# Pack products by four blocks, the last routing behind group 0, and the expert groups on two shared PSUM banks

## The chip, the cores and the metric

The kernel runs on one core of one Trainium2 chip. The metric is the device time of one execution in microseconds (us), as the median of several runs. Engines are named as in the profile: PE is TensorE's matmul stream and PEld its weight loads, DVE is VectorE, ACT is ScalarE, POOL is GpSimd, SP is SyncE, whose queue issues most DMAs. PSUM has eight banks of 128 x 512 fp32.

## What is computed

Three layers in a chain, the first from q, k, v and 32 packed queries p (8 batches, 8 heads, 576 positions, width 64):

```
p_packed = softmax(p k^T / 8) v;  x = softmax(q p_packed^T / 8) p_packed    # 4608 tokens x 512
h = relu(x @ w_in);  x = (h * h) @ w_out               # 512 -> 2048 -> 512, weights are float64
logits = x @ w_gate + modality_bias[modality_id]
e = argmax(logits);  gate = softmax(logits)[e]
out[token] = gate * (relu(x[token] @ w1[e]) @ w2[e])   # 8 experts, 512 -> 1024 -> 512
```

All of it is held to fp32 accuracy: most operands are split in two parts, hi and lo, and each product is made as hi*hi + hi*lo + lo*hi, three matmuls.

## The kernel before, in words

**Front.** The packed attention `att1` (L288 and after) runs over 16 pairs (batch, half of the heads). A front loop near the end of the file advances up to four of them by a step each tick, and every other tick pulls `conversions()`, which loads a 1 MB piece of the float64 weights, turns it into fp32 with one ACT and four DVE operations, and, for `w_out`, splits it by ACT and POOL. Pieces not converted in the front are converted in the main loop's unit 0, one per tick.

**Main loop.** Twelve units `u` of 384 tokens, in each 16 ticks `f` (128 hidden columns of 2048). A tick is `layer1` (matmuls at L455 on attention weights `a2T` and a block of the packed product), the activations (L464 to L468), and `layer2` of the tick before (L475, nine or so matmuls into three `acc` banks). The packed product is `pw(b, q)` (L359): for batch `b` and columns 256q to 256q+255 of `w_in`, eight fp32 matmuls of 64 rows, 32 columns and 256 moving columns (L365) into a pair of PSUM banks named `two`, then one ACT copy (L376) and one DVE subtraction (L377) that leave two blocks in `ring`, a ring of 20 blocks, 18 of them in one tile and two in `rtail`. `ahead()` says after which tick which `pw` is written. While the units run, `tail(u)` (L490 to L513) forms the gate logits of a unit, 24 DVE operations at L496, and `route()` (L522 to L647) puts its tokens on expert lists: its last step makes `om` and `od` on DVE and, from them, `pl` on PE (L640), one matmul per tile of 128 tokens. `tables()` (from L653) turns lists into the row indices of the gathers and scatters.

**Groups.** Nine groups of 512 tokens, each of one expert. `gathered(g)` fetches the rows by four indirect DMAs on POOL's queue (`xg`, L731) and turns them by 16 PE transposes (`tr`, L745) in PSUM banks "t"; ACT (L748) and DVE (L749) split them into `xt`. `group(g)` makes eight blocks `h` (L765, 12 matmuls of 128x512 each), evacuated by ACT (L775) and DVE (L776) into `ht`; then four output tiles `o` (L787, 24 matmuls each) into "acc" banks, scaled on DVE (L796) and scattered from POOL's queue (L798). Meanwhile SP loads the next expert's weights into two `raw` buffers (L708, L716) and ACT and DVE split them (L701, L702): four pieces of 1024 columns for w1 (`wb`) and eight of 512 for w2 (`ring`). Every third `h` block sits in the bank "h" of one pool, the others in the two banks of pool `h3`; three accumulators, two "t" banks, these three: all eight are used.

**Order.** The code is written with generators, but the Tile framework's scheduler sets the final order of each engine by its own simulated timeline and the priorities in the code; each engine then works strictly in that order.

Of the kernel before, what the change touches and what calls it, by code (L numbers as in the profile page):

```python
# [20 lines left out]
P = 128  # L21
# [5 lines left out]
def tile_pack_attention_moe_moe2(  # L27
# [191 lines left out]
    def conversions():  # L219
# [12 lines left out]
        for n in range(2):  # L232
            load(n)
        for n, (kind, u) in enumerate(CV):
            raw = raw_of(n).rearrange("p (f t) -> p f t", t=2)
# [23 lines left out]
    def bank(tag, name):  # L259
        if tag == "acc":  # L260
            return held["acc_p"].tile([P, 512], F32, tag="acc", name=name)
        return held["ps"].tile([P, 512], F32, tag=tag, name=name, bufs=held["bufs"][tag])

# [94 lines left out]

    def pw(b, q):  # L359
        ph = banks("pw")  # L360
        for g, j in ((0, 0), (2, 1), (2, 0), (0, 1), (1, 0), (3, 1), (3, 0), (1, 1)):
            c = g // 2
            o = (j + c) % 2 * NPK
            r = (2 * (g % 2)) * NPK + o
            nc.tensor.matmul(  # L365
                ph[r : r + NPK, c, : 2 * P],
                pp32[j * D : (j + 1) * D, b, g, o : o + NPK],
                w_in[q // 4 * HP + g][j * D : (j + 1) * D, q % 4 * 2 * P : (q % 4 + 1) * 2 * P],
                start=True,
                stop=True,  # L370
                tile_position=(j * D, r),
            )
        t = blocks(block(b, 2 * q), 2)
        src = ph[:, :, : 2 * P].rearrange("p c (k f) -> p k c f", k=2)
        hi = t[:, :, 0]
        nc.scalar.activation(out=hi, in_=src, func=AF.Copy)  # L376
        nc.vector.tensor_tensor(out=t[:, :, 1], in0=src, in1=hi.bitcast(F32), op=ALU.subtract)  # L377

# [344 lines left out]
    def gathered(g):  # L723
# [18 lines left out]
        for c in range(NDC):  # L742
            tp = bank("t", "tr")
            for t in range(NTT):
# [8 lines left out]
    def group(g, more):  # L753
# [4 lines left out]
        for f in range(NFE):  # L758
            if f % 2 == 0:
                pull(w2s)  # L760
            ph = bank("h", "h3") if f % 3 == 2 else held["h3"].tile([P, 512], F32, tag="h3", name="h3")
            i = 0
# [80 lines left out]
    def ahead(pair, k, f):  # L843
        late = {2 * m + 1: m + 2 for m in range(6)}
        if k == 0:
            b, q = (0, late.get(f)) if pair == 0 else (0, None)
            if q is not None:
                pw(b, q)
            b, q = 2 * pair + 1, {12: 0, 14: 1}.get(f)
        elif k == 1:  # L850
            b, q = 2 * pair + 1, late.get(f)
        else:
            b, q = 2 * pair + 2, (late | {0: 0, 2: 1}).get(f)
        if q is not None and b < B:
            pw(b, q)

# [85 lines left out]
    for i in range(len(quads) + 4):  # L942
        if i < len(quads):
            runs.append(att1(i))
        for r in (runs if i < 4 else runs[:1] + runs[:0:-1]):
            next(r)
        if i >= 4:
            runs.pop(0)
        if i % 2 and i < len(quads):
            pull(cv)  # L950
        if i == 6:
            bg = [att2(0)]
        pull(bg)
        if i >= len(quads):
            pw(0, i - len(quads)) if i < len(quads) + 2 else None
    pull(bg, 100)
# [10 lines left out]
    second_layer()  # L967
    other = [tail(NUN - 1), route(NTL - UT, NTL)]
    pull(other, 100)
    st3.close()  # L970
    held["h"] = ctx.enter_context(tc.tile_pool(name="h", bufs=NFE, side="left"))
    tables(G_A, G_MAX)

    for g in range(G_ALL):
        with tc.high_priority(offset=200 if g == 0 else 0):
            group(g, g + 1 < G_ALL)
    total = nc.values_load(ge_i[0:1, G_MAX : G_MAX + 1], min_val=0, max_val=G_MAX)

# [62 lines left out]
```

## Time and profile before

| | us |
|---|---|
| median of 3 runs (lowest, highest) | 1341.38 (1341.34, 1341.47) |
| the profiled execution: its own time | 1340.63 |
| its span, first to last instruction | 1338.8 |
| PE busy in it | 1252.5 (94%) |
| DVE, ACT, POOL busy | 773.2, 559.3, 175.5 |

The trace divides the span into the front (0 to 107 us), the main loop (to 870 us, when the last `acc` matmul ends) and the groups (870 to 1339 us, the first of them already mixed with the last ticks of the main loop). Read it from PE: a stretch in which PE is busy throughout gets shorter only by less PE work, a stretch with PE idle gets shorter by removing the wait. The lines called waits say how long an engine stood idle and which instruction released it.

### The profile page before, as it was taken

What the parts mean: (1) busy time and instruction counts of PE and PEld (TensorE: products, weight loads), DVE (VectorE), ACT (ScalarE), POOL (GpSimd) and SP (SyncE); (2) the same over time, 40 slices, a digit from 0 to 9 for tenths busy, and PEclk for the clock granted to TensorE, in tenths of its full rate; (3) what the DMA queues carried; (4) which work ended last, traced back from release to release, by engine and by line L of the source; (5) the groups of instructions that cost most, each with busy time, mean ns of one, the idle gap of its engine ahead of it and who ended that gap; (6) DMA issues with size and microseconds to landing.
All of it is one profiled execution on the core that took longest, in us unless ns stands there. A gap on an engine that the chain in (4) does not pass through costs nothing.

```text
span 1338.8 us, 19978 instructions
## 1 busy us (share of the span) xinstructions
PE 1252.5 (94%) x7572; PEld 985.0 (74%) x7572; DVE 773.2 (58%) x2008; ACT 559.3 (42%) x1061; POOL 175.5 (13%) x225
## 2 busy tenths in 40 slices
PE   5768999999999999999999999995999999999995
PEld 3546677778877878887778778874778778778774
DVE  5786654577375737764774778687243443443431
ACT  3445644554444555444444546523132332332320
POOL 4214610001000000000000010100122122122101
PEclk8787999999999999999999999997989999999997
DMA  9973300001000000010001021515142442443310
GB/s 356 369 251 127 118 17 33 9 25 33 33 33 17 24 25 33 16 49 9 26 25 41 1 88 39 157 56 177 41 144 79 149 154 77 149 159 107 122 56 34
DMA packets 56634, 115.79 MB, mean 86 GB/s; under 512 B 4432, under 2 KB 24016, under 8 KB 55376
## 3 DMA queue, kind: packets, MB, share of 16 engines
q1 hardware_dynamic: 50768, 95.25, 21.1%
q0 software_dynamic: 5760, 19.17, 4.3%
q8 instruction: 61, 1.00, 0.3%
q14 instruction: 45, 0.37, 0.1%
HBM read 95.24 MB, written 19.17 MB: 85 GB/s over the span
## 4 chain that ended last, share of the span: by engine, by line
PE 84%; DVE 6%; DMA 5%; ACT 2%; issue 2%; POOL 1%; POOLq 0%; SPq 0%; ACTq 0%; DVEq 0%
PE acc L475 29%; PE ph L455 16%; PE h L765 14%; PE o L787 13%; PE pw L365 4%; DMA xg<-x_d,idx_g 3%; PE s L410 2%; DMA wraw<-in_moe_w 1%; PE tr L745 1%; PE s L302 1%; PE pv L334 1%; PE ta L324 1%; DVE wi L244 1%; DVE ring L702 1%; PE ta L437 1%
## 5 line engine op out<-in xcount | busy, mean ns | idle before, releaser
L475 PE MATMUL acc<-wb,ghl 128*128 128x512 f32 x1728 | 447.7, 401 | 0.2 <-ACT ghl L466 0.2
L475 PEld LDWEIGHTS acc<-wb,ghl 128*128 128x128 f32 x1728 | 314.7, 189 | 80.8 <-issue 9.9
L455 PE MATMUL ph<-a2T,ring 128*128 128x384 f32 (+1 forms) x1392 | 237.3, 312 | 1.3 <-DVE pp L352 0.7
L455 PEld LDWEIGHTS ph<-a2T,ring 128*128 128x128 f32 x1392 | 208.2, 191 | 25.5 <-issue 12.8
L787 PE MATMUL o<-ring,ht 128*128 128x512 f32 x864 | 219.8, 400 | 3.5 <-ACT ht L775 3.2
L765 PE MATMUL h<-xt,wb 128*128 128x512 f32 x864 | 219.0, 402 | 0.5 <-ACT xt L748 0.5
L496 DVE SCALAR_TENSOR_TENSOR rows<-rows,wgb 128x512 f32<-128x512 f32 x288 | 199.4, 692 | 4.7
L765 PEld LDWEIGHTS h<-xt,wb 128*128 128x128 f32 x864 | 164.9, 192 | 40.8 <-ACT xt L748 1.1
L787 PEld LDWEIGHTS o<-ring,ht 128*128 128x128 f32 x864 | 161.5, 189 | 41.9 <-ACT ht L775 4.1
L464 ACT ACTIVATE r<-ph 128x384 f32<-128x384 f32 x192 | 94.2, 491 | 213.5 <-PE ph L455 198.1
L468 DVE TENSOR_TENSOR ghl<-r,ghl 128x384 fp32r<-128x384 f32 x176 | 98.6, 560 | 116.9 <-ACT ghl L466 113.2
L430 POOL TENSOR_TENSOR e<-e,sm 128x256 f32<-128x256 f32 x36 | 28.2, 782 | 597.6 <-ACT ghl L466 233.2
L466 ACT ACTIVATE ghl<-r 128x384 fp32r<-128x384 f32 x192 | 100.7, 524 | 5.7
L465 ACT ACTIVATE r<-r 128x384 f32<-128x384 f32 x192 | 100.9, 525 | 5.1
L796 DVE TENSOR_SCALAR wgb<-o,gt 128x512 f32<-128x512 f32 x36 | 27.0, 750 | 122.9 <-PE o L787 110.4
L776 DVE SCALAR_TENSOR_TENSOR ht<-h,ht 128x512 fp32r<-128x512 f32 x72 | 48.4, 687 | 56.3 <-ACT ht L775 56.3
L748 ACT ACTIVATE xt<-tr 128x512 fp32r<-128x512 f32 x36 | 21.4, 597 | 141.2 <-PE tr L745 136.5
L798 POOL DMA_INDIRECT out<-wgb,idx_s x36 | 38.8, 1078 | 297.5 <-DVE wgb L796 249.6
L775 ACT ACTIVATE ht<-h 128x512 fp32r<-128x512 f32 x72 | 40.9, 594 | 77.7 <-PE h L765 73.7
L365 PE MATMUL pw<-wi,pp 64*32 64x256 f32 x1024 | 70.3, 392 | 3.2 <-ACT eb L315 2.4
L376 ACT ACTIVATE ring<-pw 128x512 fp32r<-128x512 f32 x58 | 34.5, 596 | 86.8 <-PE ph L455 82.6
L702 DVE TENSOR_TENSOR wb<-wraw,wb 128x1024 fp32r<-128x1024 f32 x36 | 44.1, 1224 | 35.9 <-ACT wb L701 34.5
(186 smaller groups left out, 1092.2 us busy)
## 6 DMA issues: line engine op xcount, KB each, us to landing
wraw<-in_moe_w SPq DMA_DIRECT2D x72, 512.0 KB, 3.6
x_d<-rows SPq DMA_DIRECT2D x12, 792.0 KB, 3.5
qT<-in_q SPq DMA_DIRECT2D x36, 256.0 KB, 2.8
eb<-in_v SPq DMA_DIRECT2D x16, 512.0 KB, 8.0
eb<-in_k SPq DMA_DIRECT2D x11, 576.0 KB, 8.1
wgb<-in_moe_w_out SPq DMA_DIRECT2D x6, 1024.0 KB, 4.9
wgb<-in_moe_w_in SPq DMA_DIRECT2D x5, 1024.0 KB, 9.0
ec<-in_moe_w_in SPq DMA_DIRECT2D x3, 1024.0 KB, 8.3
```

Source lines behind the costliest of these rows:

```text
L365: nc.tensor.matmul(ph[r : r + NPK, c, : 2 * P], pp32[j * D : (j + 1) * D, b, g, o : o + NPK], w_in[q // 4 * HP + g][j * D : (j + 1) * D, q ...
L455: nc.tensor.matmul(ph[:, off : off + n], t[:, x, c, :], a[:, y, c, off : off + n], start=(i == 0), stop=(i == 3 * NPC - 1),)
L464: nc.scalar.activation(out=r, in_=ph, func=AF.Relu)
L465: nc.scalar.activation(out=r, in_=r, func=AF.Square)
L466: nc.scalar.activation(out=hl[:, 0], in_=r, func=AF.Copy)
L468: eng.tensor_tensor(out=hl[:, 1], in0=r, in1=hl[:, 0].bitcast(F32), op=ALU.subtract)
L475: nc.tensor.matmul(acc[t], hl[:, x, t * P : (t + 1) * P], w_out(f)[:, y, :], start=(f == 0 and x == 0 and y == 0), stop=(f == NF - 1 and x ...
L496: nc.vector.scalar_tensor_tensor(out=junk, in0=row[:, t, :DM], scalar=1.0, in1=wgb[:, e], op0=ALU.mult, op1=ALU.mult, accum_out=one)
L702: nc.vector.tensor_tensor(out=t[:, 1, :], in0=raw, in1=t[:, 0, :].bitcast(F32), op=ALU.subtract)
L765: nc.tensor.matmul(ph, half1(g % 2, c)[:, x, f * P : (f + 1) * P], xs[c][:, y, :], start=(i == 0), stop=(i == 3 * NDC - 1),)
L776: nc.vector.scalar_tensor_tensor(out=h[:, 1, :], in0=ph, scalar=0.0, in1=h[:, 0, :].bitcast(F32), op0=ALU.max, op1=ALU.subtract)
L787: nc.tensor.matmul(po, hs[f][:, x, t * P : (t + 1) * P], second(f)[:, y, :], start=(i == 0), stop=(i == 3 * NFE - 1),)
```

## The change

1. `conversions()` stops once (`yield`) behind its first two loads, and the front loop pulls it at tick 1 and at the odd ticks from 3 to 18, instead of every odd tick to 15.
2. `pw(b, f, n)` takes `n` blocks of 128 columns. `ahead()` asks for four at a time for the even batches and for the first four blocks of odd ones, for two elsewhere. A call whose blocks cross from the ring's main tile into `rtail` evacuates in two parts. The calls go from 64 to 44 (20 of four blocks, 24 of two).
3. `route()` of the last tokens and the `tables()` of the later groups are written behind group 0 instead of ahead of it. `tail()` of the last unit stays ahead.
4. Every `h` block takes one of the two banks of `h3`; the transposes `tr` of groups 1 to 8 take a bank of `h3` as well instead of a "t" bank.

```diff
@@ conversions
         for n in range(2):
             load(n)
+        yield
@@ bank
+        if tag == "h3":
+            return held["h3"].tile([P, 512], F32, tag="h3", name=name)
@@ pw
-    def pw(b, q):
+    def pw(b, f, n):
...
-                ph[r : r + NPK, c, : 2 * P],
+                ph[r : r + NPK, c, : n * P],
...
-                w_in[q // 4 * HP + g][j * D : (j + 1) * D, q % 4 * 2 * P : (q % 4 + 1) * 2 * P],
+                w_in[f // 8 * HP + g][j * D : (j + 1) * D, f % 8 * P : (f % 8 + n) * P],
...
-        t = blocks(block(b, 2 * q), 2)
-        src = ph[:, :, : 2 * P].rearrange("p c (k f) -> p k c f", k=2)
-        hi = t[:, :, 0]
-        nc.scalar.activation(out=hi, in_=src, func=AF.Copy)
-        nc.vector.tensor_tensor(out=t[:, :, 1], in0=src, in1=hi.bitcast(F32), op=ALU.subtract)
+        i = block(b, f)
+        for k0, k1 in ((0, n),) if i + n <= MOST or i >= MOST else ((0, MOST - i), (MOST - i, n)):
+            t = blocks(i + k0, k1 - k0)
+            src = ph[:, :, k0 * P : k1 * P].rearrange("p c (k f) -> p k c f", f=P)
+            hi = t[:, :, 0]
+            nc.scalar.activation(out=hi, in_=src, func=AF.Copy)
+            nc.vector.tensor_tensor(out=t[:, :, 1], in0=src, in1=hi.bitcast(F32), op=ALU.subtract)
@@ gathered
-            tp = bank("t", "tr")
+            tp = bank("h3" if g else "t", "tr")
@@ group
-            ph = bank("h", "h3") if f % 3 == 2 else held["h3"].tile([P, 512], F32, tag="h3", name="h3")
+            ph = bank("h3", "h3")
@@ ahead
-        late = {2 * m + 1: m + 2 for m in range(6)}
+        two = {2 * m + 1: (2 * m + 4, 2) for m in range(6)}
+        four = {4 * m + 3: (4 * m + 4, 4) for m in range(3)}
         if k == 0:
-            b, q = (0, late.get(f)) if pair == 0 else (0, None)
-            if q is not None:
-                pw(b, q)
-            b, q = 2 * pair + 1, {12: 0, 14: 1}.get(f)
+            b, q = 2 * pair + 1, {12: (0, 4)}.get(f)
+            if pair == 0 and f in (1, 5, 9):
+                b, q = 0, (f + 3, 4)
         elif k == 1:
-            b, q = 2 * pair + 1, late.get(f)
+            b, q = 2 * pair + 1, two.get(f)
         else:
-            b, q = 2 * pair + 2, (late | {0: 0, 2: 1}).get(f)
+            b, q = 2 * pair + 2, (four | {0: (0, 4)}).get(f)
@@ the front loop
-        if i % 2 and i < len(quads):
+        if i % 2 and 3 <= i < len(quads) + 3:
+            pull(cv)
+        if i == 1:
             pull(cv)
...
-        if i >= len(quads):
-            pw(0, i - len(quads)) if i < len(quads) + 2 else None
+        if i == len(quads):
+            pw(0, 0, 4)
@@ behind the main loop
-    other = [tail(NUN - 1), route(NTL - UT, NTL)]
-    pull(other, 100)
+    pull([tail(NUN - 1)], 100)
...
-    tables(G_A, G_MAX)
...
             group(g, g + 1 < G_ALL)
+        if g == 0:
+            pull([route(NTL - UT, NTL)], 100)
+            tables(G_A, G_MAX)
```

The lines shift by up to eight in the new file: `tr` L745 is L750, `h` L765 is L770, `ht` L776 is L781, `o` L787 is L792, the scaling L796 is L801, `pl` L640 is L645, the weight split L702 is L707, `xt` L749 is L754.

What that makes of the order shows first on PE, at the last routing's matmuls `pl` (of `om` and `od`). Before, they stand between group 0's last `o` and group 1's first `h`, with `tr` of group 1 behind the first of them (the numbers in names are buffers):

```order
L787 MATMUL o_9027<-ring,ht 128x512 x17
L640 LDWEIGHTS om
L640 MATMUL pl<-od,om 128x184
L745 MATMUL tr<-ident,xg 128x128 x4
L640 LDWEIGHTS om
L640 MATMUL pl<-od,om 128x184
L640 LDWEIGHTS om
L640 MATMUL pl<-od,om 128x184
L765 MATMUL h_9071<-xt,wb_1114 128x512
```

And after, on PE, where all of group 1's transposes and its first `h` blocks have gone by, between its third and fourth `h` block:

```order
L770 MATMUL h_8913<-xt,wb_1103 128x512 x12
L792 MATMUL o_9034<-ring,ht 128x512
L792 MATMUL o_9075<-ring,ht 128x512
L792 MATMUL o_9124<-ring,ht 128x512
L792 MATMUL o_9034<-ring,ht 128x512 x2
L792 MATMUL o_9075<-ring,ht 128x512 x2
L792 MATMUL o_9124<-ring,ht 128x512 x2
L645 LDWEIGHTS om
L645 MATMUL pl<-od,om 128x184
L645 LDWEIGHTS om
L645 MATMUL pl<-od,om 128x184
L770 MATMUL h_8935<-xt,wb_1103 128x512 x12
```

The routing's matmuls, which stood ahead of every `h` of group 1, have moved behind three of its `h` blocks and nine `o` products.

The second place is PE at the passage from a group to the next. Before, the last group's output `o_9377` and the next group's three first blocks `h_9421`, `h_9437`, `h_9459` are mixed, and the transposes of the group after that stand among them:

```order
L787 MATMUL o_9377<-ring,ht 128x512 x22
L765 MATMUL h_9421<-xt,wb_1113 128x512
L765 MATMUL h_9437<-xt,wb_1113 128x512
L765 MATMUL h_9459<-xt,wb_1113 128x512
L787 MATMUL o_9377<-ring,ht 128x512
L765 MATMUL h_9421<-xt,wb_1113 128x512 x2
L765 MATMUL h_9437<-xt,wb_1113 128x512 x2
L765 MATMUL h_9459<-xt,wb_1113 128x512 x2
L745 MATMUL tr<-ident,xg 128x128 x4
L787 MATMUL o_9377<-ring,ht 128x512
L745 MATMUL tr<-ident,xg 128x128 x4
L787 MATMUL o_9596<-ring,ht 128x512 x2
```

And after, at the same passage on PE, the last output tile `o_9515` runs through in one piece, the last four transposes follow, then the next group's `h` blocks one by one:

```order
L792 MATMUL o_9384<-ring,ht 128x512
L792 MATMUL o_9425<-ring,ht 128x512
L750 MATMUL tr<-ident,xg 128x128 x4
L792 MATMUL o_9474<-ring,ht 128x512
L750 MATMUL tr<-ident,xg 128x128 x4
L792 MATMUL o_9515<-ring,ht 128x512 x24
L750 MATMUL tr<-ident,xg 128x128 x4
L770 MATMUL h_9559<-xt,wb_1103 128x512 x12
L770 MATMUL h_9575<-xt,wb_1103 128x512 x12
L792 MATMUL o_9734<-ring,ht 128x512 x2
L792 MATMUL o_9775<-ring,ht 128x512 x2
```

The transposes of one gather no longer stand ahead of work that needs nothing from it.

The third place is DVE at that passage, which frees the `h` banks. Before:

```order
L702 TENSOR_TENSOR ring<-wraw,ring 128x512 x6
L776 SCALAR_TENSOR_TENSOR ht<-h_9421,ht 128x512
L796 TENSOR_SCALAR wgb<-o_9377,gt 128x512
L776 SCALAR_TENSOR_TENSOR ht<-h_9437,ht 128x512
L776 SCALAR_TENSOR_TENSOR ht<-h_9459,ht 128x512
L702 TENSOR_TENSOR ring<-wraw,ring 128x512 x2
L702 TENSOR_TENSOR wb_1114<-wraw,wb_1114 128x1024
L776 SCALAR_TENSOR_TENSOR ht<-h_9475,ht 128x512
```

After, on DVE, at the passage from group 0 to group 1:

```order
L754 TENSOR_TENSOR xt<-tr,xt 128x512 x2
L707 TENSOR_TENSOR ring<-wraw,ring 128x512 x4
L801 TENSOR_SCALAR wgb<-o_9165,gt 128x512
L754 TENSOR_TENSOR xt<-tr,xt 128x512
L707 TENSOR_TENSOR ring<-wraw,ring 128x512 x4
L781 SCALAR_TENSOR_TENSOR ht<-h_9209,ht 128x512
L781 SCALAR_TENSOR_TENSOR ht<-h_9225,ht 128x512
L707 TENSOR_TENSOR wb_1103<-wraw,wb_1103 128x1024 x2
L781 SCALAR_TENSOR_TENSOR ht<-h_9247,ht 128x512
```

The first `ht` of a group, which frees its `h` bank, now stands behind the scaling of the last output tile and four splits of the next weights, where before it stood ahead of that scaling.

## Rows read from the trace of the kernel before

**Rows 1.** The page: span, and the chain that ended last, by engine.

```profile
span 1338.8 us, 19978 instructions
...
PE 84%; DVE 6%; DMA 5%; ACT 2%; issue 2%; POOL 1%; POOLq 0%; SPq 0%; ACTq 0%; DVEq 0%
```

**Rows 2.** Table by stretch: window, length, busy PE PEld DVE ACT POOL, PEclk, DMA share, GB/s.

```profile
120.00:150.00 30.00, 29.36 (x188) 22.12 (x187) 21.61 (x28) 20.53 (x40) 21.28 (x16) 1.00 0.26 88
...
200.00:400.00 200.00, 200.00 (x1274) 157.93 (x1273) 124.86 (x375) 96.98 (x199) 7.52 (x9) 1.00 0.08 25
```

**Rows 3.** The same table by groups: the last routing, then two of seven periods.

```profile
915.00:930.00 15.00, 2.25 (x9) 1.46 (x9) 13.64 (x32) 5.86 (x7) 0.17 (x1) 0.53 0.54 167
...
947.03:1001.32 54.29, 51.03 (x217) 40.82 (x216) 18.86 (x27) 14.30 (x24) 8.93 (x12) 0.94 0.27 88
...
1241.50:1293.25 51.75, 51.23 (x225) 40.98 (x224) 22.15 (x30) 16.21 (x25) 5.26 (x5) 1.00 0.32 105
```

**Rows 4.** PE's waits, 870 to 1293 us: instruction, releaser, total us, times, longest.

```profile
PE pl L640 <- DVE od L632: 15.0, 2, 14.0
PE tr L745 <- DMA xg<-x_d,idx_g: 14.0, 9, 2.0
```

**Rows 5.** Timeline of PE from the last layer-2 matmuls into group 1: start, us, instruction.

```profile
868.32 2.27 PE L475 MATMUL acc<-wb,ghl 128*128 128x512 f32 x9
873.31 1.20 PE L787 MATMUL o<-ring,ht 128*128 128x512 f32 x4 [2.72 <-ACT ht L775]
...
947.03 1.33 PE L765 MATMUL h<-xt,wb 128*128 128x512 f32 x5
```

**Rows 6.** Timeline of PE at a boundary between groups.

```profile
979.88 0.60 PE L745 MATMUL tr<-ident,xg 128*128 128x128 f32 x4
980.23 5.37 PE L787 MATMUL o<-ring,ht 128*128 128x512 f32 x22
...
990.57 0.44 PE L745 MATMUL tr<-ident,xg 128*128 128x128 f32 x2 [1.98 <-DMA xg<-x_d,idx_g]
992.29 0.69 PE L745 MATMUL tr<-ident,xg 128*128 128x128 f32 x2 [1.28 <-DMA xg<-x_d,idx_g]
...
994.49 4.44 PE L765 MATMUL h<-xt,wb 128*128 128x512 f32 x12
```

**Rows 7.** A piece of the critical chain: start us, us, what.

```profile
894.06 14.00 PE o L787 x60
```

**Rows 8.** Timeline of PE: fp32 matmuls of 288 columns, then two pieces of pw.

```profile
39.23 1.19 PE L302 MATMUL s<-eb 128*64 128x288 f32 x8
40.25 0.28 PE L346 MATMUL pq<-ident,eb 128*64 128x64 f32 x4
...
303.18 0.64 PE L365 MATMUL pw<-wi,pp 64*32 64x256 f32 x8
303.75 2.37 PE L475 MATMUL acc<-wb,ghl 128*128 128x512 f32 x9
...
313.84 0.62 PE L365 MATMUL pw<-wi,pp 64*32 64x256 f32 x4
314.39 0.96 PE L475 MATMUL acc<-wb,ghl 128*128 128x512 f32 x3
```

**Rows 9.** Timeline at 1241 us: PE's `h`, ACT and DVE that free banks.

```profile
1241.48 8.56 PE L765 MATMUL h<-xt,wb 128*128 128x512 f32 x36
...
1247.64 0.58 ACT L775 ACTIVATE ht<-h 128x512 fp32r<-128x512 f32 x1
1247.77 1.23 DVE L702 TENSOR_TENSOR wb<-wraw,wb 128x1024 fp32r<-128x1024 f32 x1 [1.35 <-ACT wb L701]
1248.91 0.68 DVE L776 SCALAR_TENSOR_TENSOR ht<-h,ht 128x512 fp32r<-128x512 f32 x1
```

**Rows 10.** Landing of the gathers, from the answer on tile xg.

```profile
DMA to landing us min/median/max: 3.6/4.4/6.4
```

**Rows 11.** The page's row on the loads of w_out: KB each, median us to landing.

```profile
wgb<-in_moe_w_out SPq DMA_DIRECT2D x6, 1024.0 KB, 4.9
```

More of the change, by code (lines that the diff above doesn't have):

```diff
@@ L843, in ahead @@
     def ahead(pair, k, f):
-        late = {2 * m + 1: m + 2 for m in range(6)}
+        two = {2 * m + 1: (2 * m + 4, 2) for m in range(6)}
+        four = {4 * m + 3: (4 * m + 4, 4) for m in range(3)}
         if k == 0:
-            b, q = (0, late.get(f)) if pair == 0 else (0, None)
-            if q is not None:
-                pw(b, q)
-            b, q = 2 * pair + 1, {12: 0, 14: 1}.get(f)
+            b, q = 2 * pair + 1, {12: (0, 4)}.get(f)
+            if pair == 0 and f in (1, 5, 9):
+                b, q = 0, (f + 3, 4)
         elif k == 1:
-            b, q = 2 * pair + 1, late.get(f)
+            b, q = 2 * pair + 1, two.get(f)
         else:
-            b, q = 2 * pair + 2, (late | {0: 0, 2: 1}).get(f)
+            b, q = 2 * pair + 2, (four | {0: (0, 4)}).get(f)
         if q is not None and b < B:
-            pw(b, q)
+            pw(b, *q)
     R_ATT = 0.75
```

## The prediction

> **What bounds the kernel now.** I read the page first. The chain of work that ended last lies on PE for 84%, and only 5% and 6% on DMA and DVE [rows 1]. So the question for each edit is whether it shortens PE's work or one of its waits, and where PE waits at all. The table by stretch answers that: from 200 to 400 us PE is busy for all 200 us (the rows of 400 to 600 and 600 to 800 say the same), and even in unit 0, where conversions run, it is busy 29.36 of 30 us [rows 2]. In the main loop only less PE work can pay. In the groups there are holes: 2.25 us of work in the 15 us from 915 to 930, and 51.03 of 54.29 in group 1's period [rows 3]. The list of PE's waits names two causes: 15.0 us for the last routing's `od`, nearly all of it one wait of 14.0 us, and 14.0 us in nine pieces for gathered rows ahead of a transpose [rows 4]. A wait also costs afterwards: after the hole the granted clock is 0.94 in group 1 instead of 1.00 [rows 3], and 12 products of `h` take 994.49 to 998.76, 4.27 us, behind a gather wait [rows 6], where twelve take 2.80 at the price below. That is the second of TensorE's two levels, 1.2 GHz, for a few us.
>
> The price of PE's work in the groups: 60 products in 14.00 us, 0.2333 each [rows 7]; four transposes 980.23 - 979.88 = 0.35, so 0.0875 each [rows 6]. A group holds 8 x 12 + 4 x 24 = 192 products and 16 transposes: 44.8 + 1.4 = 46.2 us. All sums below are made against the profiled execution, 1340.63 us; the median is 0.75 higher.
>
> **The change, part by part.**
>
> *A. Transposes at the boundaries.* Before, the first transposes of the group after next stand at the head of a group, hoisted among work that needs nothing of that gather, which has only just been issued (landing 3.6 to 6.4 us [rows 10]); PE, strictly in order, stands still there. After, the 16 stand late in the previous group and the gathers are long issued. From group 1's first `h` at 947.03 [rows 5] to group 8's at 1293.25 [rows 3] there are seven periods, 346.2 us, against 7 x 46.2 = 323.4 of work. The 22.8 above it is the waits and the slow clock behind them: -22.8.
>
> *B. The last routing.* From the last `acc` matmul (868.32 plus nine at 0.2333, so 870.42) to 947.03 lie 76.6 us [rows 5]. The work in it: 213 products, 49.7, and 22 transposes, 1.9; so 25.0 are lost, to the 14-us wait, the smaller ones and the clock of 0.53 in the hole [rows 3]. After, `pl` comes behind three `h` blocks and nine products of group 1, some 45 x 0.2333 = 10.5 us plus what is mixed in, about 16.8 us behind the group's start by the new order; its `od` on DVE, whose operations now run beside group 0's last and group 1's first products, would be ready at about +13. So the wait goes. What takes its place at the start of group 0 is the wait for the first `ht`, 2.72 before [rows 5]: I leave 2.0 of it (bounds 0 and 2.7). Sum: -23.0. The queues it is moved past: SP's load of the group number for the rest stands ahead of four weight loads instead of behind two, and waits on DVE's count of groups, made before; POOL gets the gathers of group 1 ahead of the scatters' end. I cost both at 0, for the weights' buffers are full at that time; else a landing, 3.6, once.
>
> *C. Pack products.* On PE `pw` shows as unbroken pieces, and a piece costs much the same whatever it holds: 303.18 to 303.75, 0.57, for four matmuls of 256 columns (two records each), 313.84 to 314.39, 0.55, for two [rows 8]. They stand in different tiles of the array and run side by side, so the price is that of one: 0.14 plus 256 columns. The column: four fp32 matmuls of 288, in pairs side by side, take 40.25 - 39.23 = 1.02 [rows 8], so 1.77 ns a column at most and 1.67 with the same 0.03 start; 256 columns make 0.43 and 512 make 0.85, and a wide piece about 0.98. In the order built, 108 pieces become 55 narrow and 26 wide: 108 x 0.565 = 61.0 against 55 x 0.565 + 26 x 0.98 = 56.6: -4.4. Bounds: a wide piece at the narrow price, -15.2; at twice it, 1.13, -0.5. I take -4.4, for the 288-column row is the nearest with more than 256. Evacuation is off the path: DVE is busy for 124.86 and ACT for 96.98 of 200 us [rows 2], and the copies get wider, not more.
>
> What the array does around such a piece is the subject of a rule of the Trainium skill ("TensorEngine Tiling (Array Packing)", Key Properties): a change of the tiling mode drains TensorE. By that alone a piece would cost the change of mode and not its columns; what that gives is the second rival. The rows here give the same price for two and four matmuls, which fits both readings.
>
> *D. Two banks for `h` and `tr`.* A new wait. Block f needs the bank of block f-2, so `ht` f-2 must be out of ACT and DVE within one block, 2.80 us, of its end. Before there were three banks, and 36 products could run in a row [rows 9]. After, the first `ht` stands on DVE behind the last output's scaling, one `xt` and four splits, all of 512 columns like the `ht` of 0.68 [rows 9]: with 0.58 of ACT ahead, 0.58 + 7 x 0.68 = 5.3 us after the group's first `h` it ends, and block 2 wants the bank at 5.6. A margin of 0.3 us. A gather or weight piece that lands late (6.4 instead of 4.4 [rows 10], 2.0 us) would show in full. Taking that at one boundary in three gives 0.7 each, eight boundaries, +5.6 (bounds 0 and 3 each, the price of the first rival).
>
> *E. Conversions.* In the front the built order of PE, ACT and DVE is the same but for some loads of SP's, so nothing moves there; in unit 0 the conversions come one tick earlier, on ACT and DVE busy 20 to 22 of 30 us [rows 2]. PE has only 0.64 of 30 to lose or win. +1, bounds -1.6 (this idle time of unit 0, with as much again in its rest, all gained) and +4.9, one load of `w_out` late by its landing [rows 11].
>
> Sum: -22.8 - 23.0 - 4.4 + 5.6 + 1.0 = -43.6; 1340.63 - 43.6 = 1297.0, and by the median **1298**.
>
> **The rivals.**
>
> *R1. Two banks too few, every group.* DVE holds the weights' splits in pairs ahead of an `ht`: two of 1.23 [rows 9]. Then `ht` is out at 2.80 + 0.58 + 2 x 1.23 + 0.68 = 6.5, the bank wanted at 5.6: 0.9 late, three times a group, 2.7; in eight groups 21.6 instead of the 5.6 taken: 1314 (1309 to 1325). For it: the new order does hold such a pair ahead of the third `ht`. Against: in the row before, single splits let PE run 36 products with no gap [rows 9].
>
> The Trainium skill ("Perfetto Trace Analysis", Matmul Optimizations) speaks against this edit outright: all eight banks are to be in use, and after the change five are. By that rule this rival would be the rule; the trace of before, with all eight used, cannot show it.
>
> *R2. The wide piece at the narrow price, or no wait for `h`.* C at -15.2 and D at 0 to 5.6: 1287 and 1281. Against: fp32 columns have a price in the 288-column row [rows 8]. This is where the rule on tiling modes would lead.
>
> *R3. The routing's wait only moves.* DVE holds 24 logit operations, the route's and the `tables` in one queue, in order: if the `od` is ready not at +13 but as late as before, `pl` stops PE in group 1 for the same 14.0 [rows 4], with the slow clock behind it some 5 more: 1298 + 19 = 1317. Against: DVE is busy for 18.86 of the 54.29 us of group 1's period [rows 3], so it has room.
>
> *R4. Slower.* With two banks and one order, a late landing holds DVE (split behind load), DVE holds `ht`, `ht` holds PE, and PE's delay holds the next buffer: a loop of one landing, at least 3.6 [rows 10], twice a group, plus the slow clock that follows each hole (1.47 for 12 products [rows 6]): 10.1 a group. It decides from (43.6 + 5.6) / 8 = 6.2 a group on; at 10.1 it gives 1298 + 8 x 10.1 - 5.6 = 1373. Against: 36 products run on with weight splits beside them [rows 9].
>
> *R5. No effect where it counts:* the holes stay because the gathers are as late relative to their transposes as before, and the routing too. The new order speaks against it. 1340.
>
> **How the numbers follow.** The measurement tells differences from about 0.2%, 1338.7 to 1344.1. Chances: the forecast 0.62 (1288 to 1309: C's bounds and D's up to 2 each); R1 0.17; R2 0.08; R3 0.06; R4 0.05; R5 0.02. The range runs from 1286 (the upper half of R2 in) to 1324 (R1 and R3 in): it leaves out half of R2, R4 and R5, and what the unknown costs add beyond. Faster: 0.62 + 0.17 + 0.08 + 0.06 = 0.93; the same 0.02; slower 0.05.
>
> **What would show it.** Right: no `pl` wait of more than 2 us; PE's waits for `xg` below 3 us in all; seven periods of about 47 us; `pw` pieces of 0.98 where 512 columns stand in them. D shows as waits of `h` for `ht`, under 8 us in all. Wrong: a list of waits where `h` for `ht` has 15 us or more (R1), `pl` above 10 us (R3), or granted clocks well under 1.00 in every group (R4). If wide pieces cost 0.57 R2 holds. If `xg` still stands in the list with ten or more microseconds, A has failed.

## The result and the profile after

| | before | after |
|---|---|---|
| median, us (lowest, highest) | 1341.36 (1337.99, 1341.47), 4 runs | 1298.31 (1293.96, 1299.59), 4 runs |
| span of the profiled execution | 1338.8 | 1292.2 |
| ratio after / before | | 0.9679, 95% interval 0.9652 to 0.9707 |

The forecast was 1298. A second set, taken with the experiments, gave 1298.53 and 0.968 (0.9643 to 0.9717). The first profiled execution was the shortest of its four, so I keep a second profile of the same kernel beside it (span 1297.1).

The page after: span and the chain that ended last, to be read against [rows 1].

```profile
span 1292.2 us, 19310 instructions
...
PE 88%; DVE 4%; DMA 3%; ACT 2%; issue 1%; POOL 0%; SPq 0%; POOLq 0%; ACTq 0%; DVEq 0%
```

PE's waits after, from 855 us to the end (instruction, releaser, total us, times, longest), the answer to [rows 4]:

```profile
PE acc L480 <- ACT ghl L471: 1.7, 1, 1.7
PE o L792 <- ACT ht L780: 0.7, 1, 0.7
PE o L792 <- DVE wgb L801: 0.2, 1, 0.2
```

Both large rows are gone: no 15.0 us for `pl`, no 14.0 us for gathered rows. The table by stretch, with the columns of [rows 2], shows two periods from a group's first `h` to the next one's, to be read against [rows 3], whose periods run from a group's fifth `h` block to the next one's:

```profile
907.29:954.05 46.76, 46.76 (x212) 37.51 (x211) 28.68 (x61) 15.43 (x23) 8.99 (x11) 1.00 0.40 136
...
1186.75:1233.24 46.49, 46.49 (x212) 37.63 (x210) 20.45 (x29) 15.91 (x24) 8.89 (x12) 1.00 0.45 137
```

PE is busy for every microsecond of both, at a granted clock of 1.00; a period was 49.5 on the average before. The timeline (start, us, instruction, idle before) of POOL, then of PE, shows why the gathers no longer matter:

```profile
1094.48 1.00 POOL L736 DMA_INDIRECT xg<-x_d,idx_g  x1 [3.04 <-PE tr L750]
...
1098.31 0.96 POOL L736 DMA_INDIRECT xg<-x_d,idx_g  x1 [0.30 <-issue]
```

```profile
1093.76 5.84 PE L770 MATMUL h<-xt,wb 128*128 128x512 f32 x24
...
1128.09 0.60 PE L750 MATMUL tr<-ident,xg 128*128 128x128 f32 x4
```

All four gathers are issued as soon as a group begins (its first `h` at 1093.76) and used only late in that group: the first transposes of their rows start at 1128.09, 33.6 us after the first gather is issued. Before, the transposes were hoisted (moved ahead in the order) to where their rows had not landed [rows 6].

### The profile page after: what moved, and what is told of

It reads as the page before. It is cut to its first block, busy times and chain, and to the rows that moved or that the text cites. A ratio compares the mean times of both kernels' runs of the same rounds, so it can differ in the third digit from the quotient of the medians.

```text
span 1292.2 us, 19310 instructions
## 1 busy us (share of the span) xinstructions
PE 1232.2 (95%) x7252; PEld 973.1 (75%) x7252; DVE 768.8 (59%) x1992; ACT 559.4 (43%) x1045; POOL 171.5 (13%) x225
## 4 chain that ended last, share of the span: by engine, by line
PE 88%; DVE 4%; DMA 3%; ACT 2%; issue 1%; POOL 0%; SPq 0%; POOLq 0%; ACTq 0%; DVEq 0%
PE acc L480 31%; PE ph L460 17%; PE h L770 16%; PE o L792 15%; PE pw L368 4%; PE s L415 2%; DMA eb<-in_k 2%; PE tr L750 1%; PE s L305 1%; DMA rows<-in_moe_w_out 1%; DMA wraw<-in_moe_w 1%; PE ta L442 1%; DVE wi L245 0%; DVE mx L316 0%; DVE tb L241 0%
## 5 line engine op out<-in xcount | busy, mean ns | idle before, releaser
L792 PE MATMUL o<-ring,ht 128*128 128x512 f32 x864 | 218.5, 398 | 0.9 <-ACT ht L780 0.7
L770 PE MATMUL h<-xt,wb 128*128 128x512 f32 x864 | 213.5, 396 | 0.0
L770 PEld LDWEIGHTS h<-xt,wb 128*128 128x128 f32 x864 | 161.4, 188 | 38.6 <-DVE ht L781 0.4
L792 PEld LDWEIGHTS o<-ring,ht 128*128 128x128 f32 x864 | 160.5, 188 | 39.3 <-ACT ht L780 1.6
L781 DVE SCALAR_TENSOR_TENSOR ht<-h,ht 128x512 fp32r<-128x512 f32 x72 | 49.3, 688 | 113.9 <-ACT ht L780 113.8
L707 DVE TENSOR_TENSOR wb<-wraw,wb 128x1024 fp32r<-128x1024 f32 x36 | 44.1, 1224 | 46.8 <-ACT wb L706 45.5
L368 PE MATMUL pw<-wi,pp 64*32 64x256 f32 (+1 forms) x704 | 65.2, 504 | 4.5 <-DVE ring L382 4.5
L706 ACT ACTIVATE wb<-wraw 128x1024 fp32r<-128x1024 f32 x36 | 38.2, 1061 | 55.3 <-DMA wraw<-in_moe_w 53.4
L381 ACT ACTIVATE ring<-pw 128x512 fp32r<-128x512 f32 (+1 forms) x42 | 31.9, 761 | 63.6 <-PE ph L460 61.0
L382 DVE TENSOR_TENSOR ring<-pw,ring 128x512 fp32r<-128x512 f32 (+1 forms) x42 | 37.3, 889 | 32.3 <-ACT ring L381 32.0
```

Source lines behind the costliest of these rows:

```text
L368: nc.tensor.matmul(ph[r : r + NPK, c, : n * P], pp32[j * D : (j + 1) * D, b, g, o : o + NPK], w_in[f // 8 * HP + g][j * D : (j + 1) * D, f ...
L707: nc.vector.tensor_tensor(out=t[:, 1, :], in0=raw, in1=t[:, 0, :].bitcast(F32), op=ALU.subtract)
L770: nc.tensor.matmul(ph, half1(g % 2, c)[:, x, f * P : (f + 1) * P], xs[c][:, y, :], start=(i == 0), stop=(i == 3 * NDC - 1),)
L781: nc.vector.scalar_tensor_tensor(out=h[:, 1, :], in0=ph, scalar=0.0, in1=h[:, 0, :].bitcast(F32), op0=ALU.max, op1=ALU.subtract)
L792: nc.tensor.matmul(po, hs[f][:, x, t * P : (t + 1) * P], second(f)[:, y, :], start=(i == 0), stop=(i == 3 * NFE - 1),)
```

## The experiments

Each stage is told apart by two marks: PE's first layer-1 matmul, and DVE's copy of an accumulator, once at the end of each unit. With these marks the profiles divide so (us; unit 0 is from the first layer-1 matmul to its copy, "units 1 to 10" from that copy to unit 10's):

| kernel | median | first layer-1 | unit 0 | units 1 to 10 |
|---|---|---|---|---|
| before | 1341.4 | 107.72 | 76.1 | 627.33 |
| after, first and second profile | 1298.3 | 101.47, 107.24 | 82.7, 82.2 | 621.99, 621.99 |
| conversions' shift only | 1340.6 | 104.39 | 76.2 | 627.32 |
| pack products only | 1341.4 | 107.10 | 82.2 | 622.00 |
| routing only | 1320.7 | 107.28 | 75.1 | 627.32 |
| banks only | 1296.6 | 102.08 | 76.1 | 627.32 |
| after, unit 0 by two blocks | 1292.4 | 106.83 | 75.2 | 621.99 |

The marks of two of these rows, DVE's copies at the end of units 0 and 10, first the second profile of the changed kernel:

```profile
189.39 0.69 DVE L491 COPY rows<-acc 128x512 f32<-128x512 f32 x1
...
811.38 0.68 DVE L491 COPY rows<-acc 128x512 f32<-128x512 f32 x1
```

Then the kernel with unit 0 by two blocks:

```profile
181.98 0.69 DVE L491 COPY rows<-acc 128x512 f32<-128x512 f32 x1
...
803.97 0.68 DVE L491 COPY rows<-acc 128x512 f32<-128x512 f32 x1
```

**Each part alone.** Four kernels, each the kernel before with one of the four parts of the change.

*The conversions' shift.*

```diff
         for n in range(2):
             load(n)
+        yield
...
-        if i % 2 and i < len(quads):
+        if i % 2 and 3 <= i < len(quads) + 3:
+            pull(cv)
+        if i == 1:
             pull(cv)
```

> The kernel before with the conversions' shift alone. In the trace of the changed kernel PE starts its first layer-1 matmul 6.3 us earlier (101.5 against 107.7) and loses about as much in unit 0 (a pack product waits 4.5 us for the ring's evacuation, PE busy 15.9 of 23 us from 107 to 130 against 22.4). Theory: both belong to the conversions' shift, so here too the first layer-1 matmul starts near 101.5 us, unit 0 takes 4 to 7 us longer, and the whole stays at 1341 +- 3. Rival 1: the earlier start is a difference between executions; then it starts at 107 to 108 and the whole is 1341 with nothing lost in unit 0. Rival 2: the loss in unit 0 belongs to the four-block pack products; then the start is at 101.5 and the whole is 1335.

Measured: 1340.64 (10 runs; 0.9999 of before, 0.9981 to 1.0016). The start was at 104.39, between the two, unit 0 took 76.2 as before, and the end did not move. So the shift does nothing that can be measured, rival 1 is right on unit 0, and the first profile's early start is no property of the changed kernel: over all profiles here it lies anywhere from 101.5 to 107.7, with the front's code the same in many of them.

*The pack products.*

```diff
-        if i >= len(quads):
-            pw(0, i - len(quads)) if i < len(quads) + 2 else None
+        if i == len(quads):
+            pw(0, 0, 4)
...
+        two = {2 * m + 1: (2 * m + 4, 2) for m in range(6)}
+        four = {4 * m + 3: (4 * m + 4, 4) for m in range(3)}
```

(and the rest of `pw` and `ahead` as in the change)

> The kernel before with pack products of four blocks alone. Theory: a wide piece costs about 1.0 us and a narrow one 0.565, 4.4 us less in all: 1337. Rival: the four-block call of unit 0 waits for the ring's evacuation (4.5 us in the changed kernel), which eats the gain: 1341, with a wait of the pack product for DVE of 4 to 5 us early in unit 0. Rival: wide pieces are cheap beside what they replace, 15 us less: 1326 (already unlikely, since wide pieces last 1.09 us in the trace of the changed kernel).

Measured: 1341.43 (10 runs; 1.0014 of before, 0.9991 to 1.0037): no gain that can be told from nothing, as the rival had it, though not by a wait at one place. Units 1 to 10 are 5.33 us shorter, and unit 0 is 6.1 longer. PE's timeline of this kernel in unit 0:

```profile
118.35 1.09 PE L365 MATMUL pw<-wi,pp 64*32 64x512 f32 x16 [0.33 <-DVE ring L379]
...
125.52 1.31 PE L457 MATMUL ph<-a2T,ring 128*128 128x384 f32 x6 [2.73 <-ACT r L466]
...
128.63 0.69 PE L439 MATMUL ta<-ident,e 128*128 128x128 f32 x2 [1.79 <-POOL e L432]
```

Holes of 1 to 3 us appear that before's unit 0 did not have, and in the table by stretch they show with their price on the clock:

```profile
108.00:130.00 22.00, 17.14 (x92) 11.85 (x91) 12.35 (x15) 9.89 (x16) 6.11 (x6) 0.73 0.39 145
130.00:160.00 30.00, 28.33 (x147) 19.86 (x145) 21.79 (x27) 18.28 (x34) 15.61 (x14) 0.88 0.16 53
```

PE is busy for 45.5 of these 52 us, at a clock of 0.73 and 0.88; the same two stretches of before have 50.4 at 0.79 and 1.00. The first profile of the changed kernel shows another face of the same thing: there the second four-block call stands 4.52 us for DVE's ring subtraction. On ACT (start, us, idle before) its cause is a conversion that waits for a weight load, with the ring's copy queued behind it:

```profile
110.03 1.12 ACT L240 ACTIVATE tb<-rows 128x1024 f32<-128x1024 f32 x1 [4.61 <-DMA rows<-in_moe_w_out]
111.04 1.02 ACT L381 ACTIVATE ring<-pw 128x1024 fp32r<-128x1024 f32 x1
```

The order of SP's queue shows why that load is late. Two loads of `w_out`, issued just ahead of the first layer-1 matmul, have changed places. Before:

```profile
106.20 0.39 SPq L230 DMA_DIRECT2D rows<-in_moe_w_out  x1
106.67 0.47 SPq L230 DMA_DIRECT2D wgb<-in_moe_w_out  x1
```

And with the pack products alone, whose edit does not touch the loads:

```profile
105.73 0.39 SPq L230 DMA_DIRECT2D wgb<-in_moe_w_out  x1
106.22 0.41 SPq L230 DMA_DIRECT2D rows<-in_moe_w_out  x1
```

The piece in `rows` is converted first. It lands 3.5 us behind the first layer-1 matmul before, and 7.3 us behind it with the pack products alone; there ACT stands 3.40 us for it, and the ring's copy stands behind that conversion. The loads have changed places in every kernel here with four-block calls in unit 0, where ACT waits 3.4 to 4.6 us, and in none of the others, where it waits 0.4 us at most. So another order of SP's queue came with the calls. In the first profile the 4.52 us lead back to this load; how much of the 6.1 it makes was not separated.

*The routing.*

```diff
-    other = [tail(NUN - 1), route(NTL - UT, NTL)]
-    pull(other, 100)
+    pull([tail(NUN - 1)], 100)
...
+        if g == 0:
+            pull([route(NTL - UT, NTL)], 100)
+            tables(G_A, G_MAX)
```

> The kernel before with the last routing behind group 0 alone; h on three banks, transposes in the other pool. In its order the routing's matmuls come between the sixth and seventh h block of group 1. Theory: the 14-us wait goes with the slow clock behind it, 23 us less, and the nine gather waits stay: 1318. Rival: only the wait itself goes, 14: 1327. Rival: the wait moves into group 1 with DVE's backlog: 1341.

Measured: 1320.74 (0.9854, 0.9827 to 0.9881), 19 us less. PE's waits from 855 us on:

```profile
PE tr L745 <- DMA xg<-x_d,idx_g: 16.1, 9, 2.4
PE o L787 <- ACT ht L775: 2.1, 2, 1.7
```

The routing's wait is gone with the slow clock behind it (the granted clock is 1.00 from 912 to 947 us), not merely moved; the gather waits all stay, 16.1 us against 14.0 [rows 4]. The time came out 3 us above the theory's, and these longer waits are some 2 of it.

*The banks.*

```diff
+        if tag == "h3":
+            return held["h3"].tile([P, 512], F32, tag="h3", name=name)
...
-            tp = bank("t", "tr")
+            tp = bank("h3" if g else "t", "tr")
...
-            ph = bank("h", "h3") if f % 3 == 2 else held["h3"].tile([P, 512], F32, tag="h3", name="h3")
+            ph = bank("h3", "h3")
```

> The kernel before with h and the transposes on two shared banks alone; the routing is written ahead of the groups as before. In its order the transposes stand late in the previous group, and the routing's matmuls too have moved behind four h blocks of group 1 although their code has not. Theory: the gather waits go, 20.3 us less as in the changed kernel, and the routing's wait goes as well by the order alone, 23 less: 1298. Rival: the order of DVE still holds the routing's inputs back, so that PE waits for them in group 1: 1321. Rival: two banks cost 2.7 us a group: 1320, with waits of h for ht of 20 us in all.

Measured: 1296.62 (0.9684, 0.9655 to 0.9713). This one part makes all of the change's gain: the others add nothing to it in sum, since what the pack products give in units 1 to 10 they lose in unit 0. PE waits for neither `pl` nor `xg`. The order has moved the routing's matmuls into group 1 although their code still stands ahead of the groups, so the routing's gain of 19 is contained in this one and does not add.

**Which half of the bank change, and the unit 0.** Three variants of the changed kernel ran beside a repetition of it.

> The changed kernel once more, as the base of the next three. Theory: 1298 +- 2, with the same stages behind the front; the first layer-1 matmul may start anywhere from 101 to 108 us, as it did in kernels whose front is the same, so the profile can read up to 6 us longer than the first one did. Rival: the start at 101.5 belongs to the changed kernel; then it shows again.

Measured: 1298.53, the first layer-1 matmul at 107.24. This profile is 41.7 us shorter than before's, with nearly the same start.

The pack products of the front and of unit 0 by two blocks, of later units by four:

```diff
-            if pair == 0 and f in (1, 5, 9):
-                b, q = 0, (f + 3, 4)
+            if pair == 0:
+                q = {12: (0, 2), 14: (2, 2)}.get(f)
+                if f in two:
+                    b, q = 0, two[f]
...
-        if i == len(quads):
-            pw(0, 0, 4)
+        if len(quads) <= i < len(quads) + 2:
+            pw(0, 2 * (i - len(quads)), 2)
```

> The changed kernel with pack products of two blocks in the front and in unit 0, as before, and of four from unit 1 on. Theory: unit 0 loses its 6 to 7 us (82.7 against 76.1) to the four-block calls, which wait for two evacuations twice as long while PE has little else to do; units 1 to 10 keep the 5.3 us that they gained: 1298.3 - 6.5 = 1292. Rival: unit 0 loses because of the shifted conversions together with these calls, or because of the gate's setup beside it: 1298.

Measured: 1292.40 (5 runs, 1291.29 to 1293.47; 0.9637 of before, 0.9608 to 0.9667), as the theory said. Unit 0 takes 75.2 and units 1 to 10 keep 621.99.

```profile
108.00:130.00 22.00, 19.85 (x141) 14.42 (x140) 14.68 (x22) 14.13 (x27) 10.61 (x10) 0.96 0.43 154
130.00:160.00 30.00, 30.00 (x192) 22.98 (x191) 21.14 (x28) 20.21 (x40) 18.93 (x17) 0.94 0.27 94
```

PE is busy for 49.9 of the 52 us, at a clock of 0.96 and 0.94, where the four-block calls left 45.5 at 0.73 and 0.88.

The transposes back in their own two banks, `h` on two:

```diff
-            tp = bank("h3" if g else "t", "tr")
+            tp = bank("t", "tr")
```

> The changed kernel with the transposes back in their own two banks; h stays on two. In its order the first transposes of the group after next again stand ahead, mixed with h and o at the head of a group. Theory: free banks for tr are what lets them be hoisted ahead of their gather's landing; so the nine or so gather waits return with the slow clock behind them, 14 + 6 us: 1318. Rival: the third h bank (blocks of h mixed three ways) was the cause: 1298, with no gather waits.

Measured: 1312.20 (0.9789, 0.9754 to 0.9824), 14 us above the changed kernel. The gather waits are back, at two thirds of before's 14.0 us (PE's waits from 855 us on):

```profile
PE tr L750 <- DMA xg<-x_d,idx_g: 9.2, 8, 1.8
PE o L792 <- ACT ht L780: 2.4, 1, 2.4
```

Direction and cause are as the theory says, the size (20) was too large: I had taken before's waits over unchanged, and with other neighbours in the order they were shorter.

`h` back on three banks, the transposes in `h3`:

```diff
-            ph = bank("h3", "h3")
+            ph = bank("h" if f % 3 == 2 else "h3", "h3")
```

> The changed kernel with h on three banks as before and the transposes in the two h3 banks. In its order four to eight transposes still stand early at some boundaries, mixed with the next group's h. Theory: with two of the three h banks shared the transposes are held back in part, so part of the gather waits return: 1305 to 1312. Rival: two banks cost h something that three would give back, 0.7 us a group: 1293.

Measured: 1299.60 (0.970, 0.9664 to 0.9736), the same as the changed kernel within the runs' spread. Both expectations missed: no gather wait came back, and the third bank gave nothing. PE's only wait from 860 us on:

```profile
PE o L792 <- ACT ht L780: 3.0, 1, 3.0
```

Transposes stand at the boundaries here too, but they are those of the group that begins there, not of the group after it, and their rows were asked for most of a period earlier. The timeline shows it for one group, from its first gather to its first transpose:

```profile
953.82 0.99 POOL L736 DMA_INDIRECT xg<-x_d,idx_g  x1 [7.11 <-issue]
...
985.85 0.60 PE L750 MATMUL tr<-ident,xg 128*128 128x128 f32 x4
```

That is 32.0 us. For groups 3 to 8 this lead parts all the profiles of this case in two: it is 6.3 to 7.5 us wherever the transposes have their own two banks, and there PE waits for rows; it is 30.7 to 33.8 us wherever they share `h3`, and there it does not. So two banks for `h` cost nothing, and the gain lies in where the transposes' banks come from.

**The least edit, and the best kernel.** The kernel before with the transposes' pool alone changed, in one line, and two lines in `bank` that let it serve that pool:

```diff
+        if tag == "h3":
+            return held["h3"].tile([P, 512], F32, tag="h3", name=name)
...
-            tp = bank("t", "tr")
+            tp = bank("h3" if g else "t", "tr")
```

> The kernel before with the transposes of groups 1 to 8 in the two h3 banks and nothing else; h keeps its third bank, the routing stays written ahead of the groups. In its order the routing's matmuls stand in group 1 between its h blocks, and the transposes late in the group. Theory: this line alone makes the groups' gain, gather waits and routing wait both gone, 43 less as with both halves of the bank change: 1297. Rival: without the routing's move or the two-bank h one of the two waits stays: 1315 to 1320.

Measured: 1297.35 (0.9685, 0.9659 to 0.9712): this one line (with the two in `bank`) makes the whole gain. PE's timeline of it shows the routing's three matmuls, none with a wait:

```profile
928.08 0.25 PE L642 MATMUL pl<-od,om 128*128 128x184 f16 x1
928.44 0.25 PE L642 MATMUL pl<-od,om 128*128 128x184 f16 x1
...
933.47 0.25 PE L642 MATMUL pl<-od,om 128*128 128x184 f16 x1
```

They run no earlier than the 926.24 at which before's first one began, and DVE ends the last `od` at 929.46, where it was 928.55 before. PE has only had other work to do meanwhile. Why the scheduler puts `pl` behind group 1's first blocks once `tr` is in another pool wasn't traced; `pl` and `tr` shared the "t" pool before, which is a guess at the link and no more.

Last, the bank change with four-block products from unit 1 on, without the conversions' shift and without the routing's move:

> The kernel before with the bank change and with pack products of four blocks from unit 1 on; neither the conversions' shift nor the routing's move. Theory: those two are worth nothing beside the others, so this equals the changed kernel with unit 0 by two (1292.4): 1291 to 1293, with units 1 to 10 in 622.0 us and unit 0 in 75 to 76. Rival: the routing's move is worth what separates them: 1294 or more, with a wait of PE for the routing or DVE's backlog in group 1.

Measured: 1292.89 (5 runs; 0.9643, 0.9621 to 0.9665), the same as the changed kernel with unit 0 by two (1292.40). So the two parts left out are worth nothing beside the others, and this kernel, some 5.5 us faster than the changed one, is a simpler one.

## Why the prediction was right, point by point

The time came out as forecast, but two of the five terms (D and E) were wrong and offset each other, and a third (C) came close in part by luck. A and B are read from the first profile of the changed kernel, C and E from the second, which starts layer 1 at 107.24 like before's 107.72:

| step | predicted | measured | how |
|---|---|---|---|
| A, gather waits at boundaries | -22.8 | -20.3 | seven periods, 907.29 to 1233.24 in the first profile, 325.95 against 346.2 |
| B, last routing | -23.0 | -23.3 | from the last `acc` to the end, -40.8 with 12 products (2.8) more to do there, less A |
| C, pack products | -4.4 | -5.3 | units 1 to 10, where the prediction's prices give -2.4 |
| D, two banks | +5.6 | 0 | no wait of `h` for `ht` |
| E, unit 0 | +1.0 | +6.1 | unit 0, 82.2 against 76.1 |
| sum | -43.6 | -42.8 | profile to profile -41.7 |

The 1.1 us between the sum and the profiles are mostly unit 11, which lost 2.0 that no step had, less a start that came 0.5 earlier; 1.8 of the 2.0 is a wait of the last `acc` for its activations (1.7 in the first profile, in the list of waits above).

Two places were misread, without harm to the sum. Before, 947.03 and 1293.25 are the starts of the fifth `h` blocks of groups 1 and 8, not of the first, which PE's timeline has at 929.41 for group 1:

```profile
929.41 1.65 PE L765 MATMUL h<-xt,wb 128*128 128x512 f32 x3 [0.49 <-ACT xt L748]
```

The seven periods hold, since both ends lie at the same place of a group, and so does B's work, which was counted to that place. And after, `pl` comes behind four `h` blocks and 24 `o` products of group 1, not behind three and nine; the 16.8 us are those 72 products at 0.2333.

**A** was right in cause and a little too large: it assumed periods of 46.2, and they are 46.5 even with PE full; the price of 0.2333 came from 60 products of one kind in a piece [rows 7], and a period has four runs of products behind transposes, each some 0.08 us longer than its products (24 of them from 948.02 to 953.70, 5.68 against 5.60).

**B** was right in size, and its assumption that the `od` would be ready held: no `pl` matmul waited, the first coming 16.8 us behind group 1's first `h`, as worked out. PE in the first profile:

```profile
907.29 5.76 PE L770 MATMUL h<-xt,wb 128*128 128x512 f32 x24
...
919.16 2.96 PE L770 MATMUL h<-xt,wb 128*128 128x512 f32 x12
...
924.07 0.33 PE L645 MATMUL pl<-od,om 128*128 128x184 f16 x2
```

What it got wrong is whose merit it is. I put it down to the moved call; the bank change alone moves `pl` as well. A and B are not two gains of two edits but one gain of one line, with a second way to its larger half.

**C** had the price of a wide piece right and left out what a piece costs its neighbours. PE's timeline of the changed kernel in unit 1, two wide pieces and what follows each, then a run of `acc` with no piece beside it:

```profile
234.06 1.06 PE L368 MATMUL pw<-wi,pp 64*32 64x512 f32 x8
235.05 2.37 PE L480 MATMUL acc<-wb,ghl 128*128 128x512 f32 x9
237.34 1.06 PE L368 MATMUL pw<-wi,pp 64*32 64x512 f32 x8
238.34 1.59 PE L460 MATMUL ph<-a2T,ring 128*128 128x192 f32 x12
...
258.20 2.25 PE L480 MATMUL acc<-wb,ghl 128*128 128x512 f32 x9
260.30 1.21 PE L460 MATMUL ph<-a2T,rtail 128*128 128x384 f32 x6
```

The pieces take 0.99 and 1.00 us from start to start, against the 0.98 worked out from the 288-column row [rows 8], so their own price is mostly columns. But nine `acc` products take 2.29 us between two pieces (235.05 to 237.34) and 2.10 without one beside them (258.20 to 260.30): a piece costs some 0.1 us more on either side, a term that the prediction put at nothing. In units 1 to 10, 92 narrow pieces have become 53 narrow and 20 wide; by the prediction's prices that is 2.4 us less, and 5.3 were measured. The 19 pieces that are gone, at up to 0.2 each, are large enough for the rest. That -4.4 for all the pieces lies near -5.3 for those of ten units is in part luck.

The Trainium skill ("TensorEngine Tiling (Array Packing)", Key Properties) states that a change of the tiling mode drains TensorE. The trace agrees as far as a piece has a price beside its columns, the 0.14 us left in it and the 0.2 around it; whether a drain makes that price no run here shows. It does not carry R2, which needs a wide piece to cost no more than a narrow one.

**D** was wrong. Its arithmetic on DVE held; its need didn't. The timeline of the changed kernel at a boundary, PE, ACT and DVE:

```profile
1047.27 5.85 PE L770 MATMUL h<-xt,wb 128*128 128x512 f32 x24
...
1051.13 0.58 ACT L780 ACTIVATE ht<-h 128x512 fp32r<-128x512 f32 x1
1051.94 0.68 DVE L781 SCALAR_TENSOR_TENSOR ht<-h,ht 128x512 fp32r<-128x512 f32 x1
...
1052.95 1.55 PE L792 MATMUL o<-ring,ht 128*128 128x512 f32 x6
...
1054.34 2.96 PE L770 MATMUL h<-xt,wb 128*128 128x512 f32 x12
1057.14 2.02 PE L792 MATMUL o<-ring,ht 128*128 128x512 f32 x8
...
1059.00 2.96 PE L770 MATMUL h<-xt,wb 128*128 128x512 f32 x12
```

The first bank is free at 1052.62, 5.35 us behind the group's first `h`, where I had 5.3. But I had the third block want it at 5.6, as if blocks followed each other. The order places six `o` products between the second and third block, so the bank is wanted at 7.07, and from then on 3.5 to 5.4 us pass from block to block in this period (4.66 in the rows shown), not 2.80. The failed step is that cover, and it could have been read from the order of PE, where the first `o` products stand right behind the first two `h` blocks. R1 fell with it.

The Trainium skill ("Perfetto Trace Analysis", Matmul Optimizations) states that all eight banks are to be in use. The runs here do not bear that out for these groups: with five in use PE runs without a gap, with six (`h` on three) the time is the same, and with seven (transposes in their own two) it is 14 us longer, by the order that the free banks allow.

**E** was wrong in size and in cause. The conversions' shift is worth 0 alone; the 6.1 us are those of the four-block calls in unit 0. The sentence of step C that failed is "Evacuation is off the path", which I had read from the stretch of 200 to 400 us, where DVE is busy 62% and PE has 200 us of queued work. In unit 0 the pack products are made just ahead of their use. The evacuation is longer (0.6 us before and 1.0 after on ACT), and it stands on ACT behind a conversion that waits for its load. In the first profile the next call then waits 4.52 us, since the two banks named `two` are one buffer; in the second, and with the pack products alone, PE's longest wait is one of 2.7 us for an activation `r` that stands on ACT behind that copy. That the four-block calls in unit 0 cost these 6 us is shown by taking them out; how the loss divides between the longer copies, the swapped loads and the rest of the order is open. The upper bound of E, one load of `w_out` that lands late, named a part of what happened, but put it down to the conversions' shift, and at +4.9 it didn't hold the 6.1.

The other rivals fell by the same rows: no wait for `pl` appeared in group 1 (R3), the granted clock is 1.00 in both periods shown above (R4), a wide piece is not cheap (R2), and the holes did not stay (R5).

The offset: D took off 5.6 us of gain that were not lost, E left out 5.1 that were, A promised 2.5 too much and C 0.9 too little. The forecast's own range (1288 to 1309) would have held without this luck, at 1303 or so with D as taken and E as measured, or 1292 with D at nothing and E as taken.

## What to carry to other kernels

Where a scheduler sets the order, a pool of free banks can be a licence to hoist: in this case work that took its bank from a shared, busy pool came late, and late was what the strictly ordered PE needed, since the rows it waits for had then landed. Count a buffer's cover in the new order with all that stands between two uses of it, not by the block alone. A price that holds where an engine has work queued (evacuation hidden) has to be worked out anew for the stage where the product is made just in time, and there the order of the other queues has to be read again too: an edit of a matmul call swapped two loads. One edit at a time shows which of several edits carries the gain: here one line, with two in a helper, of more than fifty.

## What the runs showed of the hardware that I had not expected

The front, in whose first 67 us the DMA engines are busy at a share of 0.99 (before), varies from one execution to the next: the first layer-1 matmul started between 101.47 and 107.72 us in the profiles here, 101.47 and 107.24 in two of the very same kernel. What makes it vary was not traced. What comes later is steadier: units 1 to 10 took 621.99 or 622.00 us in each of the four profiles with wide products listed above, and 627.32 or 627.33 in the four with narrow ones. So a few us in the whole time are told from the noise by stages and not by the total.
